# Attention scores as sixteen 32x32 tiles of the PE array in place of four 32x128 row tiles

## Chip, cores, metric

One core of one Trainium2 chip. The time is the device time of one execution in microseconds. All runs named here were fast (granted TensorE clock 0.995 to 1.000), except where a lower clock is named.

## The reference

Two independent attention layers whose outputs stand side by side. Each has 32 heads of 32 columns, 2048 positions, and a causal window of 256 positions.

```python
qkv = (x @ wqkv).reshape(B, S, 3, H, Dh)          # S = 2048, D = 1024, H = 32, Dh = 32
scores = einsum("bhqd,bhkd->bhqk", q, k) * Dh**-0.5
mask = (i - j >= 0) & (i - j < 256)
o = einsum("bhqk,bhkd->bhqd", softmax(where(mask, scores, -1e9)), v)
out = o.reshape(B, S, D) @ wo                      # for A and for B, then concatenated
```

## The kernel before

Four heads (128 columns of q and k) are worked on together. The 128x128 blocks of scores that the window touches are handled four at a time, in 180 "sections". A section writes the scores of its four blocks for the four heads into `st`, one PSUM bank per head; one exponential reads all four banks.

```python
def session(now):
    es = entries_of(now)                     # up to 4 blocks (g, j, q)
    st = ps_st.tile([P, 4, SLOTS, P], F32, name="st")
    ...                                      # a..b: neighbouring blocks with one key block j
        for r in range(4):                   # head r: array rows 32r..32r+31, PSUM bank r
            nc.tensor.matmul(
                st[:, r, a:b, :],
                lhsT=kT[32 * r:32 * r + 32, j * P:(j + 1) * P],
                rhs=qT[32 * r:32 * r + 32, q * P:(q + b - a) * P],
                start=True, stop=True, tile_position=(32 * r, 0))
    ...
    nc.scalar.activation(out=pt..., in_=st..., func=ACT.Exp, bias=-SHIFT, scale=cfg.scale)
```

The products with V (`pv`) use four column tiles of 128x32. The projections use one 128x128 tile, or four 128x32 column tiles where a product with V in that shape comes just before:

```python
def by_columns(out, lo, hi, lhsT, rhs, start, stop):
    if whole[0]:
        nc.tensor.matmul(out[:, lo:hi], lhsT=lhsT, rhs=rhs, start=start, stop=stop, ...)
        return
    for c in range(0, P, 32):
        nc.tensor.matmul(out[c:c + 32, lo:hi], lhsT=lhsT[:, c:c + 32], rhs=rhs, start=start,
                         stop=stop, tile_position=(0, c), skip_group_check=True)
...
for now in range(END):                       # 180 sections
    whole[0] = not (due and due[0][0] <= now)
    session(now)                             # scores
    while due and due[0][0] <= now:
        pv(pg, pk)                           # products with V, if due
    emit(now, level(now) - fixed[now])       # projections until the next section
```

About 125 sections are followed by a product with V and column-tiled projections ("dense" sections below), about 55 by whole projections ("sparse" sections).

## Time and profile before

| | before |
|---|---|
| time, median of 2 | 612.89 us |
| TensorE share of the chain that ended last | 94% |
| score line's share of that chain | 10% |
| TensorE matmuls and weight loads in the trace | 12,774 and 12,824 |

A line of the groups reads: line, engine, operation, output<-inputs, shape (array rows\*columns, then output partitions x columns), count, then busy microseconds and the mean nanoseconds of one, then idle time of the engine before them and what ended it. PE is the matmul side of TensorE, PEld its weight loads. A line of the waits reads: who waited, for whom, microseconds in all, times, the longest. "issue" means that the engine waited for nothing that the profile shows. The lines themselves stand in the prediction.

### The profile page before, as it was taken

What the parts mean: (1) busy time and instruction counts of PE and PEld (TensorE: products, weight loads), DVE (VectorE), ACT (ScalarE), POOL (GpSimd) and SP (SyncE); (2) the same over time, 40 slices, a digit from 0 to 9 for tenths busy, and PEclk for the clock granted to TensorE, in tenths of its full rate; (3) what the DMA queues carried; (4) which work ended last, traced back from release to release, by engine and by line L of the source; (5) the groups of instructions that cost most, each with busy time, mean ns of one, the idle gap of its engine ahead of it and who ended that gap; (6) DMA issues with size and microseconds to landing.
All of it is one profiled execution on the core that took longest, in us unless ns stands there. A gap on an engine that the chain in (4) does not pass through costs nothing.

```text
span 611.4 us, 28739 instructions
## 1 busy us (share of the span) xinstructions
PE 594.2 (97%) x12774; PEld 346.0 (57%) x12824; DVE 463.7 (76%) x1193; ACT 445.2 (73%) x382; POOL 328.4 (54%) x630
## 2 busy tenths in 40 slices
PE   7999999999999999999999999999999999999996
PEld 5555466656654655655565765755445664545543
DVE  1477888888799889888888889798897978897200
ACT  3777888888887877867777877777776778776332
POOL 0566566656565666655555656556565556555000
PEclk9999999999999999999999999999999999999999
DMA  9824110111015510444111010112012030114221
GB/s 237 177 71 107 38 38 4 38 38 39 3 26 88 102 37 3 82 96 106 37 29 46 16 27 2 39 36 72 11 44 57 3 106 20 55 48 129 71 78 64
DMA packets 86802, 35.47 MB, mean 58 GB/s; under 512 B 65552, under 2 KB 86160, under 8 KB 86672
## 3 DMA queue, kind: packets, MB, share of 16 engines
q1 hardware_dynamic: 85632, 33.31, 22.6%
q8 instruction: 102, 1.67, 1.2%
q10 hardware_dynamic: 1040, 0.26, 0.2%
q14 instruction: 28, 0.23, 0.1%
HBM read 17.83 MB, written 8.39 MB: 43 GB/s over the span
## 4 chain that ended last, share of the span: by engine, by line
PE 94%; ACT 2%; issue 1%; DMA 1%; DVE 1%; SPq 0%; POOL 0%; ACTq 0%
PE pp L176 43%; PE pp L172 28%; PE acc L513 13%; PE st L451 10%; ACT pt L459 2%; DMA oT<-in_A_x_dram 1%; DVE top L184 0%; DVE both L481 0%; ACT vt L190 0%; PE st L578 0%; ACT kT L190 0%; DVE rinv L524 0%; PE acc L578 0%; SPq L548 0%; POOL pt L467 0%
## 5 line engine op out<-in xcount | busy, mean ns | idle before, releaser
L459 ACT ACTIVATE pt<-st 128x2048 bf16<-128x2048 f32 x180 | 338.0, 1878 | 86.6 <-PE st L451 70.4
L471 POOL TENSOR_SCALAR_AFFINE_SELECT pt<-pt 128x512 bf16<-128x512 bf16 x224 | 155.9, 696 | 145.5 <-ACT pt L459 145.5
L467 POOL TENSOR_SCALAR_AFFINE_SELECT pt<-pt 128x512 bf16<-128x512 bf16 x256 | 179.6, 703 | 87.8 <-ACT pt L459 87.8
L176 PE MATMUL pp<-xT,wqk 128*32 128x512 bf16 x2728 | 164.2, 379 | 1.1 <-POOL wv L350 1.0
L524 DVE RECIPROCAL rinv<-acc 128x128 f32<-128x128 f32 x128 | 121.9, 952 | 56.8 <-PE acc L513 55.6
L481 DVE TENSOR_TENSOR both<-pt 128x512 bf16<-128x512 bf16 x224 | 138.3, 657 | 0.0
L176 PEld LDWEIGHTS <-wqk 128*32 128x32 bf16 x2728 | 70.0, 97 | 55.9 <-DVE both L481 1.1
L172 PE MATMUL pp<-xT,wqk 128*128 128x512 bf16 (+1 forms) x321 | 76.8, 375 | 5.1 <-issue 3.6
L176 PE MATMUL pp<-wv,xT 128*32 128x256 bf16 x2436 | 75.8, 273 | 0.0
L451 PE MATMUL st<-qT,kT 32*128 32x384 bf16 (+2 forms) x1488 | 71.6, 269 | 0.0
L176 PEld LDWEIGHTS <-xT 128*32 128x32 bf16 x2436 | 64.0, 97 | 5.3 <-issue 0.2
L529 DVE STREAM_SHUFFLE wide<-rinv 128x128 f32<-128x128 f32 x256 | 64.4, 297 | 0.0
L513 PE MATMUL acc<-pt,vt 128*32 128x128 bf16 (+1 forms) x2160 | 63.4, 240 | 0.0
L172 PE MATMUL pp<-wo_sb,oT 128*128 128x512 bf16 (+1 forms) x275 | 60.1, 373 | 1.6 <-issue 1.4
L451 PEld LDWEIGHTS <-kT 32*128 32x128 bf16 x1488 | 22.3, 92 | 65.2 <-issue 63.8
L190 ACT CAST osb<-pp 128x512 bf16<-128x512 f32 (+1 forms) x54 | 31.1, 577 | 38.3 <-PE pp L172 25.8
L531 DVE TENSOR_TENSOR oT<-acc,wide 128x256 bf16<-128x256 f32 x128 | 54.3, 425 | 4.4
L172 PEld LDWEIGHTS <-wqk 128*128 128x128 bf16 x358 | 33.6, 100 | 37.1 <-issue 6.9
L176 PE MATMUL pp<-wo_sb,oT 128*32 128x512 bf16 x928 | 54.6, 379 | 0.0
L172 PE MATMUL pp<-wv,xT 128*128 128x256 bf16 x415 | 51.0, 273 | 0.5 <-ACT kT L190 0.2
L513 PEld LDWEIGHTS <-vt 128*32 128x32 bf16 x2160 | 36.0, 96 | 26.3 <-issue 24.0
L172 PEld LDWEIGHTS <-xT 128*128 128x128 bf16 x415 | 38.9, 98 | 11.6 <-issue 5.1
(46 smaller groups left out, 382.3 us busy)
## 6 DMA issues: line engine op xcount, KB each, us to landing
out_dram<-osb SPq DMA_DIRECT2D x63, 128.0 KB, 1.8
wqk<-in_B_wqkv_dram SPq DMA_DIRECT2D x32, 128.0 KB, 2.7
wqk<-in_A_wqkv_dram SPq DMA_DIRECT2D x24, 128.0 KB, 2.9
wo_sb<-in_A_wo_dram SPq DMA_DIRECT2D x16, 128.0 KB, 2.2
wv<-in_B_wqkv_dram SPq DMA_DIRECT2D x16, 128.0 KB, 2.6
wo_sb<-in_B_wo_dram SPq DMA_DIRECT2D x16, 128.0 KB, 2.9
oT<-in_A_x_dram SPq DMA_DIRECT2D x4, 256.0 KB, 5.1
wv<-in_A_wqkv_dram SPq DMA_DIRECT2D x2, 512.0 KB, 6.1
```

What stands on the lines that cost most here:

```text
L172: nc.tensor.matmul(out[:, lo:hi], lhsT=lhsT, rhs=rhs, start=start, stop=stop, skip_group_check=True)
L176: nc.tensor.matmul(out[c:c + 32, lo:hi], lhsT=lhsT[:, c:c + 32], rhs=rhs, start=start, stop=stop, tile_position=(0, c), skip_group_check=True)
L190: nc.scalar.copy(out=out, in_=in_)
L451: nc.tensor.matmul(st[:, r, a:b, :], lhsT=kT[32 * r:32 * r + 32, j * P:(j + 1) * P], rhs=qT[32 * r:32 * r + 32, q * P:(q + b - a) * P], st ...
L459: nc.scalar.activation(out=pt[:, :, :n, :].rearrange("p r a q -> p r (a q)"), in_=st[:, :, :n, :].rearrange("p r a q -> p r (a q)"), func= ...
L467: nc.gpsimd.affine_select(out=blk, in_=blk, pattern=[[0, 4], [1, P]], compare_op=ALU.is_ge, fill=0.0, base=0, channel_multiplier=-1)
L471: nc.gpsimd.affine_select(out=blk, in_=blk, pattern=[[0, 4], [-1, P]], compare_op=ALU.is_gt, fill=0.0, base=0, channel_multiplier=1)
L481: nc.vector.tensor_tensor(out=both[:, :, h, :], in0=pts[s0][:, :, a0, :], in1=pts[s1][:, :, a1, :], op=ALU.add)
L513: nc.tensor.matmul(acc[32 * r:32 * r + 32, o:o + w_], lhsT=lhsT, rhs=src[:, r, :, :], start=(x == 0), stop=(x == len(moves) - 1), tile_pos ...
L524: nc.vector.reciprocal(out=rinv[:], in_=acc[:, 2 * P:3 * P])
L529: nc.vector.stream_shuffle(out=wide[:, h * P:(h + 1) * P], in_=rinv[:], mask=[16 * h] * 32)
L531: nc.vector.tensor_tensor(out=oTs[(pi, k)][:, t, (p % 2) * 256:(p % 2 + 1) * 256], in0=acc[:, 0:256], in1=wide[:], op=ALU.mult)
```

## The change

Every score matmul is cut along its keys: head r and keys c to c+31 of a block now use the 32x32 tile at row 32r and column c. The intent is to keep all sixteen 32x32 tiles busy with independent matmuls, in a shape with the same 32 columns as the neighbouring column tiles.

```diff
-            for r in range(4):
-                nc.tensor.matmul(
-                    st[:, r, a:b, :],
-                    lhsT=kT[32 * r:32 * r + 32, j * P:(j + 1) * P],
-                    rhs=qT[32 * r:32 * r + 32, q * P:(q + b - a) * P],
-                    start=True, stop=True, tile_position=(32 * r, 0))
+            for c in range(0, P, 32):
+                for r in range(4):
+                    nc.tensor.matmul(
+                        st[c:c + 32, r, a:b, :],
+                        lhsT=kT[32 * r:32 * r + 32, j * P + c:j * P + c + 32],
+                        rhs=qT[32 * r:32 * r + 32, q * P:(q + b - a) * P],
+                        start=True, stop=True, tile_position=(32 * r, c), skip_group_check=True)
```

## The prediction

> **What bounds the kernel now.** I read the page first: busy shares, then the chain that ended last, then the groups by line with their forms kept apart, the list of waits, and the order of time on PE and PEld around a few score sections.
>
> ```profile
> PE 594.2 (97%) x12774; PEld 346.0 (57%) x12824; DVE 463.7 (76%) x1193; ACT 445.2 (73%) x382; POOL 328.4 (54%) x630
> PE 94%; ACT 2%; issue 1%; DMA 1%; DVE 1%; SPq 0%; POOL 0%; ACTq 0%
> PE pp L176 43%; PE pp L172 28%; PE acc L513 13%; PE st L451 10%; ACT pt L459 2%; DMA oT<-in_A_x_dram 1%; DVE top L184 0%; DVE both L481 0%; ACT vt L190 0%; PE st L578 0%; ACT kT L190 0%; DVE rinv L524 0%; PE acc L578 0%; SPq L548 0%; POOL pt L467 0%
> ```
>
> TensorE carries 94% of the chain, and every other engine has a quarter of its time free. So a nanosecond added to or taken from TensorE's own sequence goes almost whole into the time. The changed line is L451, with 10% of the chain.
>
> ```profile
> L451 PE MATMUL st<-qT,kT 32*128 32x384 bf16 x448 | 37.7, 327 | 0.0
> L451 PE MATMUL st<-qT,kT 32*128 32x128 bf16 x544 | 29.6, 219 | 0.0
> L451 PE MATMUL st<-qT,kT 32*128 32x256 bf16 x496 | 25.6, 273 | 0.0
> PEld L451 <- issue: 63.8, 176, 0.7
> POOL pt L471 <- ACT pt L459: 145.5, 112, 2.7
> ACT pt L459 <- PE st L451: 70.4, 114, 1.3
> ```
>
> 448 + 544 + 496 = 1488 matmuls are 372 groups of four row tiles, in 180 score sections (the exponential that follows each section is listed 180 times). A matmul's 219 to 327 ns is a latency; what it takes from its successors is read from starts:
>
> ```profile
> 305.30 0.59 PE L172 MATMUL pp<-xT,wqk 128*128 128x512 bf16 x2
> 305.82 0.40 PE L451 MATMUL st<-qT,kT 32*128 32x128 bf16 x8
> 306.15 0.52 PE L513 MATMUL acc<-pt,vt 128*32 128x128 bf16 x16
> 306.49 0.28 PE L513 MATMUL acc<-pt,ones 128*32 128x128 bf16 x8
> 306.60 0.29 PE L513 MATMUL acc<-both,ones 128*32 128x128 bf16 x8
> 306.72 0.82 PE L176 MATMUL pp<-xT,wqk 128*32 128x512 bf16 x12
> 307.36 0.39 PE L176 MATMUL pp<-wv,xT 128*32 128x256 bf16 x8
> 305.82 0.12 PEld L451 LDWEIGHTS <-kT 32*128 32x128 bf16 x8 [0.42 <-issue]
> 306.15 0.29 PEld L513 LDWEIGHTS <-vt 128*32 128x32 bf16 x16 [0.21 <-issue]
> ```
>
> From 306.49 to 306.60 to 306.72 two groups of four column tiles with 128 columns pass each time: 0.055 us a group. From 306.72 to 307.36 three groups with 512 columns pass: 0.213 us a group. So four tiles run side by side, a group takes 0.42 ns per moving column, and 32 column-tile instructions cost no more than their stream. At a change of the tile shape this breaks. The last 128x512 matmul before the scores starts at 305.51 (305.30 plus one step) and has streamed by 305.73, yet the first score weights start at 305.82: about 95 ns with nothing. The scores (one group of 128 columns, one of 384: 0.213 us, plus some 0.02 us of first load and offsets) have streamed by about 306.06, and the next weights start at 306.15: again about 95 ns. A section therefore costs 0.33 us from 305.82 to 306.15, or some 0.42 us with the bubble before it. 180 sections x 2 bubbles x 0.095 = 34 us are drains, and 720 blocks x 128 columns x 0.42 ns = 39 us are score streaming.
>
> [...] 95 ns at each change, none between the products with V and the column-tiled projections at 306.72. [...] Here the starts of the four tiles of a group in the trace's own records lie 3 to 4 ns apart (305.825, 305.828, 305.832, 305.835)[...]; no run yet shows sixteen. [...] groups of 128x256 column tiles, eight instructions each, pass in 0.109 us for over 50 matmuls on end, 13.6 ns per instruction without a stall.
>
> **The change part by part.**
>
> *Arithmetic stream:* unchanged. Four row tiles already fill all 128 rows and 128 columns. Sixteen tiles cut the weights' columns in four, not the moving columns: every tile still streams its 128 to 384 columns. If all sixteen run together, a group still takes 0.42 ns per column. Gain: 0.
>
> *Mode changes:* still two per section. From 128x128 both dimensions would now change; from 128x32 only the rows. In the trace each kind costs alike: 128x128 to 32x128 (rows alone) 95 ns, and the one place where 128x32 goes straight to 128x128 (columns alone; last start 569.35 plus 0.053 of stream, next start 569.50) about 98 ns. I find no reason for 32x32 to 128x32 to be free. Gain: 0.
>
> *Instructions:* 1488 pairs of weight load and matmul become 5952, so 4464 pairs or 8928 instructions more, on 25,598 (12,774 + 12,824): +35%. [...] a pair takes about 3.3 ns to start (four pairs in 13 ns at 305.82). Within a section sixteen pairs take 53 ns, just the stream of a 128-column group (54 ns), so the next group isn't held up. But the last tile starts 15 x 3.3 = 50 ns after the first, where it was 3 x 3.3 = 10 ns, and the drain counts from the last tile's end. Cost: 40 ns x 180 = 7.2 us. I add about 1 us for loads at the heads of sections: the first load after a drain delays the second group by some 11 ns now (0.067 us for 128 columns against 0.055).
>
> *Weight loads:* the same 128 columns per row strip, as four loads of 32. In column mode four loads of 32 columns hide behind 0.055 us of stream; in row mode four strips load at once. If both hold together, no cost.
>
> *Off the path:* the exponential of a section starts 40 ns later; the score bank is free again well before the next section in most cases, and ACT has 27% idle. PSUM banks and partitions per tile are as before: head r in bank r. No transfers move but instruction fetch (1.67 MB now, about 0.6 MB more, 1.2% of the engines now).
>
> Sum: 612.9 + 7.2 + 1 = 621 us, +1.3%.
>
> **The rivals.**
>
> *Instruction supply becomes the bound.* A section of two groups holds 64 instructions instead of 16, and in 125 or so sections the product with V follows with 104 more in 0.57 us (5.5 ns each). [...] All the trace proves is that supply is no slower than 13.6 ns per instruction. [...] For it: the burst is dense and 35% more instructions come. Against: no stall of this kind anywhere now[...]. I give it a quarter.
>
> *Tiles or loads don't run together in the small shape.* If loads of one row strip go one after another (13 ns each as 32 columns at 0.42 ns), or each start costs more than 3.3 ns, a group takes some 200 ns whatever its width: groups of 128, 256 and 384 columns (136, 124 and 112 of them) lose about 150, 100 and 45 ns, 38 us in all: 650 us and more. Against: column tiles load within 55 ns four at a time now. One in ten.
>
> *The drain shrinks*, because 32x32 and 128x32 have the same columns: up to 250 changes x 95 ns = 24 us less, 589 to 597. Against: each single-dimension change in the trace drains in full. One in twenty-five.
>
> **Range and chances.** Three parts in five for the plain sum with a few us to either side (616 to 625), the rest mostly above. The 2% line is 625.1 us, so the supply rival alone would cross it. Predicted 621 us, range 614 to 645; faster by over 2% 0.04, within 2% 0.56, slower by over 2% 0.40.
>
> **What the changed profile would show.** Right: L451 with 5952 matmuls; in a section, starts of a group's first and last tile 50 ns apart; section starts to the next line's starts about 0.37 us in place of 0.33, still followed by about 95 ns without weight loads; products with V at 0.055 us per 128 columns, as before. Supply rival: sections normal, but gaps put down to "issue" inside the products with V or the first projections after them, groups there slower than 0.42 ns per column. Serial rival: sections of 0.5 us or more, with narrow groups taking as long as wide ones. Drain rival: the gap before the products with V under 95 ns. What would make me wrong most easily is a start cost per tile other than 3.3 ns, since it is multiplied by 15 and by 180.

## The result, and the profile after

The changed kernel took 638.84 us (median of 2, 636.79 to 640.88), against 612.89 us: ratio 1.0422, 95% interval 1.0353 to 1.0491. A ratio here is the mean time of one kernel's fast runs over that of the other's fast runs of the same rounds, so not quite the ratio of the medians.

First the page of the changed kernel: busy shares, the chain by engine and by line. Source lines below the change have moved by one, so the scores are L452 and the products with V L514.

```profile
PE 608.6 (95%) x17237; PEld 366.1 (57%) x17288; DVE 463.3 (72%) x1193; ACT 446.1 (70%) x382; POOL 325.2 (51%) x630
PE 92%; issue 3%; ACT 1%; DVE 1%; DMA 1%; SPq 0%; ACTq 0%
PE pp L176 42%; PE pp L172 27%; PE acc L514 13%; PE st L452 11%; ACT pt L460 1%; DMA oT<-in_A_x_dram 1%; DVE both L482 0%; PE st L579 0%; DVE top L184 0%; ACT kT L190 0%; DVE rinv L525 0%; SPq L549 0%; PE acc L579 0%; DVE qT L192 0%; ACT vt L190 0%
```

TensorE is still the chain. The share of "issue" has grown from 1% to 3%, and that is where to look. Next the waits that name it. In the kernel before, L176 had one such row, on PEld, and none on PE:

```profile
PEld L176 <- issue: 1.0, 3, 0.6
```

In the changed kernel:

```profile
PEld L452 <- issue: 68.8, 181, 2.0
PEld L176 <- issue: 10.7, 13, 1.7
PE pp L176 <- issue: 6.3, 7, 1.4
PE st L452 <- issue: 4.5, 5, 2.0
```

The 68.8 us ahead of the score loads (181 waits) are mostly the waits at the changes of tile shape, as before (63.8 us, 176 waits): the last matmul of 512 columns starts 307 ns ahead of the first score weights in both kernels at the median, of which 213 ns are its stream and about 95 ns are empty. The empty part is called a drain here. The other rows are new or ten times larger, and they are of another kind: few, and long. An undisturbed section looks as the prediction had it. Here is the order of time on PE in the changed kernel (start us, duration us, engine, line, operation, count; in brackets the idle time before it and what ended it):

```profile
321.74 1.24 PE L172 MATMUL pp<-xT,wqk 128*128 128x512 bf16 x4
322.91 0.44 PE L452 MATMUL st<-qT,kT 32*32 32x128 bf16 x32
323.28 0.51 PE L514 MATMUL acc<-pt,vt 128*32 128x128 bf16 x16
323.62 0.28 PE L514 MATMUL acc<-pt,ones 128*32 128x128 bf16 x8
323.73 0.29 PE L514 MATMUL acc<-both,ones 128*32 128x128 bf16 x8
```

The section takes 0.37 us where it took 0.33 us. Over all 180 sections the median went from 330 to 367 ns. The products with V run at 0.055 us per 128 columns, as before. The cost that is not in this picture is here, in the same view of two other stretches:

```profile
119.76 0.61 PE L176 MATMUL pp<-xT,wqk 128*32 128x512 bf16 x8
120.29 0.29 PE L452 MATMUL st<-qT,kT 32*32 32x256 bf16 x6
122.06 0.42 PE L452 MATMUL st<-qT,kT 32*32 32x256 bf16 x26 [1.47 <-issue]
...
225.76 0.71 PE L176 MATMUL pp<-wv,xT 128*32 128x256 bf16 x17
227.88 0.40 PE L176 MATMUL pp<-wv,xT 128*32 128x256 bf16 x7 [1.41 <-issue]
```

TensorE stops in the middle of a group, after 6 of 32 score matmuls or after 17 column-tile matmuls (not even a multiple of four), and goes on more than a microsecond later without anything having been released to it. The stops go with the instruction's place in the program, whatever the instruction is. Counting TensorE's records from the start and setting the instruction queue's transfers beside them gives this table, worked out from the trace's records of the changed kernel:

```
instruction no.  steps of 256 since   last start -> next start   page transfer that ran then
                 the row above        us                         us
 6324            -                    120.31 -> 122.06           119.62 to 120.54
 8880            10, less 4           163.36 -> 164.41           161.81 to 163.12
12710            15, less 10          226.20 -> 227.88           225.52 to 226.48
21132            33, less 26          368.92 -> 370.00           367.40 to 368.83
23432             9, less 4           406.50 -> 408.20           405.93 to 406.88
29817            25, less 15          516.60 -> 517.94           515.54 to 516.42
```

The stops come at multiples of 256 instructions (the small shortfalls, 59 in some 23,500 records, may be instructions that the trace does not list: it has 51 matmuls fewer than weight loads). At each, a transfer of the instruction queue had started 0.6 to 1.6 us before the stop, and TensorE went on 1.2 to 1.5 us after that transfer had ended. The page lists that queue so, first in the kernel before, then in the changed one:

```profile
q8 instruction: 102, 1.67, 1.2%
```

```profile
q8 instruction: 137, 2.24, 1.5%
```

Each packet is 16,384 bytes, and 35 packets for 8,928 more instructions are 255 instructions a packet. From these counts and the table I take it to be TensorE's own program, arriving in pages of 256 instructions. In the changed kernel no two pages were fetched less than 3.3 us apart, however fast the instructions were used. Seven stops of 0.9 to 2.0 us (the six of the table and one at 27.2 us) make 10.1 us, and some seventeen shorter ones another 6.1 us.

The traces also show how the pages follow each other. A fetch does not follow the one before it at once. Run 10 below has 82 stops of over 0.3 us at page ends, and after each of them the next fetch started only when TensorE had been back at work for a while: 1.05 to 1.9 us (the middle nine tenths; median 1.2). From the start of a fetch to TensorE going on with that page it took 2.2 to 3.4 us (median 2.4). One after the other the medians make 3.6 us. The shortest time between two fetches is 3.1 to 3.4 us in each of the twelve traces, so 3.3 us is the fastest page seen and not the usual one: the fetches that the six stops of the table waited for came 3.3 to 4.5 us after the fetch before.

So the theory for the experiments (A): about 8 us come from the sections themselves and 16 us or more from **instruction pages** that arrive no faster than one per 3.3 us. The rivals: (B) the 32x32 shape is slow in itself, in loading, starting or draining; (C) the pages are late because data transfers share the transfer engines with them; (D) each added instruction costs the same, wherever it stands.

### The profile page after: what moved, and what is told of

It reads as the page before. It is cut to its first block, busy times and chain, and to the rows that moved or that the text cites. A ratio compares the mean times of both kernels' runs of the same rounds, so it can differ in the third digit from the quotient of the medians.

```text
span 639.1 us, 37666 instructions
## 1 busy us (share of the span) xinstructions
PE 608.6 (95%) x17237; PEld 366.1 (57%) x17288; DVE 463.3 (72%) x1193; ACT 446.1 (70%) x382; POOL 325.2 (51%) x630
## 4 chain that ended last, share of the span: by engine, by line
PE 92%; issue 3%; ACT 1%; DVE 1%; DMA 1%; SPq 0%; ACTq 0%
PE pp L176 42%; PE pp L172 27%; PE acc L514 13%; PE st L452 11%; ACT pt L460 1%; DMA oT<-in_A_x_dram 1%; DVE both L482 0%; PE st L579 0%; DVE top L184 0%; ACT kT L190 0%; DVE rinv L525 0%; SPq L549 0%; PE acc L579 0%; DVE qT L192 0%; ACT vt L190 0%
## 5 line engine op out<-in xcount | busy, mean ns | idle before, releaser
L176 PE MATMUL pp<-xT,wqk 128*32 128x512 bf16 x2728 | 165.7, 379 | 2.1 <-DVE both L482 1.2
L176 PEld LDWEIGHTS <-wqk 128*32 128x32 bf16 x2728 | 74.0, 97 | 54.2 <-issue 2.5
L452 PE MATMUL st<-qT,kT 32*32 32x384 bf16 (+2 forms) x5952 | 82.0, 270 | 4.5 <-issue 4.5
L176 PE MATMUL pp<-wv,xT 128*32 128x256 bf16 x2436 | 77.9, 273 | 5.7 <-issue 5.7
L452 PEld LDWEIGHTS <-kT 32*32 32x32 bf16 x5952 | 37.7, 88 | 71.0 <-issue 68.8
L176 PEld LDWEIGHTS <-xT 128*32 128x32 bf16 x2436 | 64.6, 97 | 12.4 <-issue 7.9
L514 PE MATMUL acc<-pt,vt 128*32 128x128 bf16 (+1 forms) x2160 | 64.8, 239 | 0.8 <-issue 0.6
L176 PE MATMUL pp<-wo_sb,oT 128*32 128x512 bf16 x928 | 54.7, 379 | 0.0
L514 PEld LDWEIGHTS <-vt 128*32 128x32 bf16 x2160 | 36.8, 95 | 23.5 <-issue 21.4
L172 PEld LDWEIGHTS <-oT 128*128 128x128 bf16 x288 | 27.3, 98 | 31.5 <-issue 1.0
```

What stands on the lines that cost most here:

```text
L452: nc.tensor.matmul(st[c:c + 32, r, a:b, :], lhsT=kT[32 * r:32 * r + 32, j * P + c:j * P + c + 32], rhs=qT[32 * r:32 * r + 32, q * P:(q + b ...
L514: nc.tensor.matmul(acc[32 * r:32 * r + 32, o:o + w_], lhsT=lhsT, rhs=src[:, r, :, :], start=(x == 0), stop=(x == len(moves) - 1), tile_pos ...
```

## The experiments

Ten kernels ran; all gave correct results. The kernel before was run beside each: 612.1 to 612.6 us.

### 1. As many instructions, without any 32x32 tile (row_halves)

```diff
-            for r in range(4):
-                nc.tensor.matmul(st[:, r, a:b, :], ..., rhs=qT[.., q * P:(q + b - a) * P], ...
+            for s in range(2 * (b - a)):                 # halves of 64 columns
+                for r in range(4):
+                    nc.tensor.matmul(st[:, r, a + s // 2, 64 * (s % 2):64 * (s % 2) + 64], ...,
+                                     rhs=qT[.., q * P + 64 * s:q * P + 64 * s + 64], ...
```

> Scores stay in the old 32x128 row tiles, but every 128-column block is issued as two matmuls of 64 columns: 5760 pairs of load and matmul in place of 1488, nearly the 5952 of the change, with no 32x32 tile anywhere. Theory A (instruction supply: TensorE's instructions arrive in pages of 256, a page at most every 3.4 us or so, and where more are used TensorE stands still at a page boundary): stalls as in the changed kernel, 12 to 20 us of them, no late last tile, so 625 to 634 us, with gaps put down to issue at instruction counts 256 apart. Theory B (the 32x32 shape itself is slow to load, start or drain): 612 to 617 us and no such gaps.

Measured: 630.09 us, ratio 1.0281 (1.0248 to 1.0315). This kernel has no 32x32 tile, and two thirds of the loss are there. The order of time on PE in this run:

```profile
217.28 0.41 PE L454 MATMUL st<-qT,kT 32*128 32x64 bf16 x32
...
218.07 0.28 PE L516 MATMUL acc<-both,ones 128*32 128x128 bf16 x5
219.38 0.24 PE L516 MATMUL acc<-both,ones 128*32 128x128 bf16 x3 [1.03 <-issue]
```

The same stop, now after 5 of 8 matmuls of a product with V, which nobody had touched. Its stops are again 256 instructions apart, but they sum to only some 9 us, below the 12 to 20 expected; sections take 345 ns instead of 330 (2.7 us in all), and one wait of 2.6 us for VectorE, 1.1 us in the kernel before, is longer. These make some 13 of 17.7 us; the rest was not traced. B falls as the cause of the larger part.

### 2 and 3. The change with few instructions around it (before_whole, after_whole)

All projections as single 128x128 matmuls, without the change and with it (a second assignment to `whole[0]`, after the last section, was taken out as well):

```diff
-        whole[0] = not (due and due[0][0] <= now)
+        whole[0] = True
```

> Kernel before with all projections as single 128x128 matmuls: some 9,100 instructions fewer, about 127 further changes of tile shape after the products with V. Both theories: 127 x 0.095 us = 12 us more, 623 to 627 us. It is the base for the next run.

> Changed kernel with all projections as single 128x128 matmuls: sixteen 32x32 tiles for the scores, but about as many TensorE instructions as the kernel before. Theory A: no page stalls left, so only the 37 ns per section (6.7 us) over the run with whole projections and row tiles: 629 to 634 us. Theory B: the whole 26 us over it: 647 to 653 us.

Measured: 626.10 us (1.0220) and 634.52 us (1.0356). The base lies 13.7 us above the kernel before, near the 12 us of 127 further drains. On it the change costs 8.4 us, not 26, with the same sixteen tiles in all 180 sections. The time lies 0.5 us above A's range and 12 us below B's. The waits of the second run have no long "issue" left:

```profile
PEld L452 <- issue: 64.5, 177, 0.7
PEld L514 <- issue: 20.8, 115, 0.4
```

The 8.4 us are a little more than 180 x 37 ns = 6.7 us. The rest is in the twelve sections with three groups of blocks, which take 0.52 to 0.58 us instead of 0.33. One of them in the order of time on PE of that run:

```profile
82.82 0.65 PE L452 MATMUL st<-qT,kT 32*32 32x128 bf16 x48
83.40 0.40 PE L514 MATMUL acc<-pt,vt 128*32 128x128 bf16 x12
```

Its 48 pairs are 96 instructions. In the trace's records 65 of them (32 pairs and one weight load) start within 0.12 us, then nothing starts for 0.13 us, then a pair follows every 8.3 ns. That is 4.2 ns per instruction. All twelve such sections of this run pause after the 65th; why was not tested. Those twelve sections cost some 12 x 0.2 = 2.4 us beyond their 37 ns each, so 9.1 us by the trace against 8.4 us timed.

### 4. Eight tiles of 32x64 (tiles_32x64)

```diff
-            for c in range(0, P, 32):
+            for c in range(0, P, 64):          # and c + 64 in place of c + 32
```

> Eight tiles of 32x64: 2976 pairs. Theory A: last tile starts 7 x 3.3 ns after the first in place of 3 x 3.3, so 13 ns x 180 = 2.4 us, plus 0 to 4 us of page stalls as only 12% more instructions come: 614 to 620 us. Theory B: if the cost is of small tiles in general, about a third to a half of the 26 us: 622 to 626 us; if of 32x32 alone, 612 to 615 us.

Measured: 618.60 us, 1.0107 (1.0081 to 1.0134), inside A's range. Sections take 354 ns: 24 ns more than before, not the 13 that seven start steps give. With one long stop of about 1 us left, the loss is mostly in the sections. The trace shows where the further 11 ns lie: the second group of a section starts 11 ns later than before (82 ns after the section's start in place of 71, where the first group has 128 columns). With sixteen tiles it does not (68 ns). Why it does with eight was not tried.

### 5 and 6. The change in part of the sections (small_where_whole, small_where_cols)

```diff
+        w_ = 32 if whole[0] else P             # or: 32 if not whole[0] else P
-            for c in range(0, P, 32):
+            for c in range(0, P, w_):          # and c + w_ in place of c + 32
```

> Sixteen 32x32 tiles only in the sections that whole 128x128 projections follow (about 55 of 180), row tiles in the others. Theory A (page supply): 55 x 37 ns = 2.0 us for the late last tiles and next to no page stalls, since few instructions follow there: 613 to 617 us. A theory in which every added instruction costs the same: 55/180 of 26 us = 8 us, 620 to 622 us.

> Sixteen 32x32 tiles only in the sections that a product with V and column-tiled projections follow (about 125 of 180). Theory A: 125 x 37 ns = 4.6 us, some 2 us for the few sections of more than two groups, and most of the page stalls of the changed kernel, 10 to 16 us: 629 to 637 us. Equal cost per added instruction: 125/180 of 26 us = 18 us, 630 to 632 us, so this run says little alone, and something together with the other.

Measured: 616.34 us (1.0055) and 627.28 us (1.0237). The sparse 55 sections cost 4.2 us in place of D's 8. Of these 1.7 us are one stop, 29 us into the kernel, where the second page comes more than 7 us after the first in this kernel and in the one before alike; 2.7 us are the sections, by the trace. The dense 125 cost 15.2 us, a little less than A expected: by the trace some 6 us of it in the sections and 6 to 7 us in page stops; the other 2 to 3 us were not traced. The two parts sum to 19.4 us, not to 26. That fits A and not D. Why the parts sum to less than the whole these runs do not show.

### 7. More instructions where few are used (before_cols)

Scores as before, all projections up to the last section in column tiles, so 5,068 more instructions in the parts that had been whole:

```diff
-        whole[0] = not (due and due[0][0] <= now)
+        whole[0] = False
```

> Kernel before, scores untouched, with every projection in column tiles: about 5,000 TensorE instructions more, in the parts that had been whole. Theory A: the demand rises where it had been low, to 13.6 ns per instruction at most, which is 3.5 us per page of 256 against 3.3 to 3.5 us at the fastest page spacing: few stalls, 0 to 5 us: 612 to 618 us. If it is the number of instructions and not their density: 5,000 of 8,900 times 18 us = 10 us, 622 to 624 us.

Measured: 613.21 us, ratio 1.0004 (0.9974 to 1.0033). Five thousand instructions cost nothing that can be told from zero. D falls.

### 8. More data traffic (after_traffic)

The changed kernel with a further 96 KB load into an unused tile after every load piece:

```diff
             f()
+            nc.sync.dma_start(out=junk[0][:], in_=wsrc(0)[:, 0:3, 0, 0:P])
```

> Changed kernel with a further load of 96 KB into an unused tile after each load piece: about 25 MB of traffic on top of 33 MB, results unchanged, TensorE's instructions unchanged. Theory C (the instruction pages come late because data transfers share their DMA engines): clearly more stalls, 645 us or more. Theory A (a page has a shortest spacing of its own, whatever the traffic): 636 to 642 us.

Measured: 710.26 us, at a granted clock of 0.954 in the profiled run. That lies in C's range, but as a test by time this failed, since the real loads came late too:

```profile
PE pp L177 <- DMA wqk<-in_A_wqkv_dram: 33.9, 3, 20.6
```

TensorE waited 33.9 us for weights in three places (and more for x), and its granted clock was 0.86 to 0.90 in the stretches with these waits (50 to 100 and 200 to 400 us) against 0.97 to 1.00 in the others. The pages themselves can still be read from the trace. Their transfers took 1.03 us at the median (1.11 us in the changed kernel), the closest two fetches were 3.3 us apart, and the stops at page ends sum to about as much as without the traffic. And the pages can be sorted by what else was moving: 46 page transfers ran while data moved at over 100 GB/s and took 0.97 us at the median, 57 ran with under 10 GB/s and took 1.03 us. In the changed kernel it is 0.97 us (25) against 1.10 us (84). Data traffic did not make the pages slower, so C finds no support; a run with more traffic and all data on time was not made.

### 9. Denser projections instead of scores (proj_halves)

Scores as before; each 512-column projection matmul as two of 256, half after half:

```diff
-                chains.append(_Chain(early, late, qk_steps(g, which, k)))
+                st_ = {}
+                chains.append(_Chain(early, late, qk_steps(g, which, k, 0, 256, st_, last=False)
+                                     + qk_steps(g, which, k, 256, 512, st_)))
```

(and the same in the output projection)

> Kernel before with its scores untouched, but every query, key and output projection matmul of 512 columns issued as two of 256: about 8,400 TensorE instructions more (the change adds 8,928), no new tile shape and no further change of shape. They fall where the products with V already use many. Theory A (pages of 256 instructions, 3.4 to 4.1 us each where TensorE waits for them): a section with a product with V holds some 16 + 104 + 150 = 270 instructions in 3.0 us, more than a page gives (3.6 to 4.3 us), so long runs of stalls: 650 to 720 us. If only the number counts: 8,400 of 8,928 times 18 us = 17 us, 628 to 632 us. Theory B (the 32x32 shape): 612 to 616 us.

Measured: 621.74 us, 1.0149 (1.0120 to 1.0179), outside all three ranges. The direction is A's (stops at page ends, about 5 of the 9.3 us; the rest was not traced), the size is not. The count was wrong: the trace has 233 instructions per dense section on average, not 270. That is 13.3 ns per instruction on average and never below 12.4, while a page of 256 in 3.3 us gives 12.9. The demand is about that of the fastest page. In the changed kernel the average is 14.2, but a tenth of the dense sections run at 11.4 ns or less, and once 600 instructions on end, more than two pages, pass in 6.2 us, 10.3 ns each.

### 10. Both together (after_proj_halves)

The sixteen tiles of the change on top of run 9.

> Both at once: the changed kernel's sixteen 32x32 tiles and the halved projection matmuls of the run before it. Counted this time in the traces: a section with a product with V has 226 TensorE instructions in the changed kernel on average, and halving the projections added 56, so 282 in some 3.1 us, 11 ns each. Theory A with pages of 256 instructions no faster than 3.3 us each (12.9 ns per instruction): 282 x 12.9 = 3.64 us, so 0.5 us x 125 sections = 66 us over the kernel before if the sections with few instructions can't be used to catch up, up to twice that if a page on which TensorE waits takes 4 us; 665 to 740 us, with page fetches steadily 3.3 to 4.2 us apart. If the costs of the two changes just add up: 26 + 9 = 35 us, 645 to 651 us.

Measured: 695.05 us, ratio 1.1335 (1.1307 to 1.1363). Added up, the two changes would have cost 35 us; together they cost 82 us, inside the range that the page pace gives. The waits of this run:

```profile
PEld L176 <- issue: 39.9, 48, 1.6
PE pp L176 <- issue: 28.4, 41, 1.4
PE st L456 <- issue: 11.2, 21, 1.2
```

They are the waits of the changed kernel, only many more of them. The page fetches now follow each other steadily. Of 169 intervals eight in ten lie between 3.45 and 4.35 us, the median is 3.75 us, and the shortest is 3.26 us.

## Why the prediction was right or wrong

The measured time lies in the stated range, and the side of the 2% line was given 40% against 56% for the other. The central figure, 621 us, was 18 us low, and the plain sum with its few us to either side (616 to 625) missed. The range holds the result because it was stretched for the supply rival, whose mechanism was not the one that the runs show. So much of the hit is luck.

- **Stream and drains unchanged: right.** Products with V pass at 0.055 us per 128 columns, and the bubbles of about 95 ns stand before and after the scores as they did. Going from 32x32 to 128x32, which have the same columns, is not free: where the last group has 384 columns, the next weights start 250 ns after its last tile, against 249 ns before. So the change had nothing to win.
- **Late last tile, 40 ns a section: right.** 37 ns measured, and the last tile of a section starts 37 ns later in the trace (118 ns after the first weight load in place of 81, where the first group has 128 columns). By runs 2 and 3 it is 8.4 us against the 7.2 + 1 of the sum, but the 1 us agrees by luck. It did not come from first loads as written (the second group starts no later than before): some 2 us come from the twelve sections of 96 instructions, which pause for 0.13 us after the 65th in run 3.
- **Instruction supply at zero, the step that failed.** The sum has no term for it. The prediction looked for a rate at which single instructions are taken, and that rate was no limit here: 4.2 ns in run 3. The limit was in the term that the prediction waved through under transfers that move ("instruction fetch", 1.2% of the engines). The share of the engines was small, and still is at 1.5%. What counts is the time from one page to the next: 3.3 us at the fastest, 12.9 ns per instruction, and 3.75 us or 14.6 ns at the median of run 10. The missing term is 16 us.
- **The supply rival: right in direction, wrong in mechanism.** It put the time above the 2% line of 625.1 us, within a range that ends at 645, and gave it a quarter. The supply over several pages is 12.9 ns per instruction at the fastest page and 14.6 ns at the median of run 10, but it comes in steps of 256, so the gaps are few and long, and they stand wherever a page ends: in scores, products with V or projections alike. Its expected place, inside the products with V or just after them, was too narrow.
- **Serial tiles and a shorter drain: wrong, as weighted.** A section of a 128-column and a 384-column group takes 367 ns, as one of two 256-column groups does, so narrow groups are not held up; and run 1 loses most of the time without any small tile.
- **Start steps of 3.3 ns: right.** The starts of sixteen tiles lie 50 ns apart from first to last in the changed kernel, 3.3 ns a step.

The parts add up to 8.4 + 16.2 = 24.6 us of 26.0. The profiled execution, 27.7 us longer than the one before, had a granted clock of 0.997 against 0.999, which would be, as an estimate from these two figures, about 1 us more. The remaining microsecond or two were not traced.

## What to carry to other kernels

Cutting the score matmuls into more tiles gained nothing here, since four row tiles already covered all 128 rows and columns and the stream stayed as long (250 ns from the last tile of a 384-column group to the next weights, against 249), and each further instruction was a claim on a supply that gave one page of 256 instructions per some 3.3 us at the fastest and per 3.75 us at the median when TensorE waited for it again and again (run 10). Count the instructions of the densest few microseconds, not of the whole program: 5,000 more cost nothing where demand was low, 8,900 more cost 26 us where it was high (some 16 us of it in page stops), and two such changes cost more together than apart. Stops that follow no wait, cut through the middle of a group and lie multiples of 256 instructions apart are the sign of it.
